# First batch of attention: p turned by plain transposes, reciprocals of the sums multiplied into x by GpSimd

## Chip, cores and metric

One core of one Trainium2 chip. The metric is the device time of one launch in microseconds, as the median over runs. The engines are PE (TensorE, matmuls), DVE (VectorE), ACT (ScalarE), POOL (GpSimd) and SP (SyncE, which issues most of the transfers).

## What is computed

A thresholded attention over 8 batches, 8 heads, 576 rows and a head size of 64, and after it a gated feed-forward block on 4608 rows of 512, with 1536 inner columns. All is float32; the weights arrive as float64 and are taken apart on the chip.

```python
scores = scale * np.matmul(q, k.transpose(0, 1, 3, 2))
thresh = np.max(scores, axis=-1, keepdims=True) - tau
scores = np.where(scores >= thresh, scores, -1000000000.0)
attn = np.exp(scores - np.max(scores, axis=-1, keepdims=True))
attn = attn / (np.sum(attn, axis=-1, keepdims=True) + 1e-09)
x = np.matmul(attn, v)          # then (B,H,S,D) -> (B*S, H*D)
g = x @ w_gate
out = (g * (1.0 / (1.0 + np.exp(-g))) * (x @ w_val)) @ w_out
```

## The kernel before

The kernel has two parts. The first batch is written out by hand, in the order in which the program issues its instructions; the seven others are handed out by a planner (`Plan`), which keeps a modelled time for each engine and places jobs by the durations that stand in their calls. Engines run their own instructions strictly in that order.

The first batch has four pairs of heads and, in each, five tiles of query rows: four of 128 and one of 64. The tiles 0 and 1 ("early", `t < TA`) of all four pairs come first, as their rows of x feed the first unit of the feed-forward block; the tiles 2, 3 and 4 follow, pair by pair. Beside them the weights are brought into float32 piece by piece: ACT splits (L322, L323), POOL clamps (L315), DVE shifts (L342) and joins (L348), POOL adds the lower part (L358). From the second round on, PE fills in gate and value matmuls of the first unit (L580), with the tanh halves copied by ACT (L595, L596), the value product on DVE (L604) and the gate product on POOL (L611).

One tile passes through these steps. PE makes the scores of both heads in the two PSUM tiles `sc` (L462, L468 for the last tile). DVE takes the negated maxima (L479), ACT the exponentials into p (L482) and the threshold (L484), DVE masks p and sums it (L487), adds the sums up and takes the reciprocals `ri` (L489, L490). While the next tile is in its first steps, p is turned: PE writes four blocks of 128 columns for each head to a PSUM bank `tp`, and the 64 columns left over of both heads to a bank `end`; ACT copies them to `pT` and `pT2` (L540, L544, L547). One tile later PE multiplies with v (`attend_tile`, L564, L566) into a bank `xa`, from which ACT copies x to its place (L569), the moving operand of the gate matmuls.

The division by the sums happens in one of two ways. For early tiles the turning is a true matmul against the identity scaled by `ri` (ACT makes it, L503; PE at L533 and L537). For the others p itself is scaled, one head by ACT (L497), the other by POOL (L495), and turned by plain transposes (L531, L539); for the scores of the second head there, the key columns start 64 further on (`turned`), so that the 64 columns left over of both heads lie side by side and one transpose turns both.

The four PSUM banks for `tp`, `end`, `xa`, `pg` and `pv` go round in the order in which they are given back (`bank`, `give_back`). A bank is written again only when its last reader is done; so are the two `sc` tiles, which DVE's mask reads last.

In the planned part two tiles of the first batch are still attended, in its first two groups; the second goes through the planner as a job of ACT.

Of the kernel before, what the change touches and what calls it, by code (L numbers as in the profile page):

```python
# [13 lines left out]
AF = mybir.ActivationFunctionType  # L14
ALU = mybir.AluOpType
# [113 lines left out]
def kernel(  # L129
# [105 lines left out]
    def room(n):  # L235
        nonlocal at
        at += n
        return pall[:, at - n:at]
# [6 lines left out]
    dbufs = deque(room(2 * P).rearrange("p (h q) -> p h q", h=2) for _ in range(2))  # L245
# [199 lines left out]
    heads = [slice(h * D, (h + 1) * D) for h in range(2)]  # L445

    def turned(t):
        return TA <= t < NT

    def statistics(*names):  # L450
        return [stp.tile([P, 2 * MU, 2] if x == "mx" else [P, 2 * MU], F32, name=x) for x in names]
# [1 line left out]
    def scores(seg, t):  # L453
        qT, kT = seg["qT"], seg["kT"]
        q0 = t * P - seg["q0"]
        if t < NT:
            pss = [next_sc() for _ in range(2)]
            for h, hs in enumerate(heads):
                cut_ = D if turned(t) and h == 1 else 0
                for n, lo, to in [(0, 0, D), (0, D, SH), (1, 0, SH)] if cut_ else [(0, 0, SH), (1, 0, SH)]:  # L460
                    at_ = (n * SH + lo - cut_) % S
                    nc.tensor.matmul(pss[h][:, n, lo:to], qT[hs, q0:q0 + P], kT[hs, at_:at_ + to - lo],  # L462
                                     start=True, stop=True)
        else:
            pss = [next_sc()]
            for n, h in ((0, 0), (1, 1), (1, 0), (0, 1)):
                hs = heads[h]
                nc.tensor.matmul(pss[0][hs, n, 0:SH], qT[hs, q0:q0 + D], kT[hs, n * SH:(n + 1) * SH],  # L468
                                 start=True, stop=True)
        nm, th, ri, tot = statistics("nm", "th", "ri", "tot")  # L470
        sm = sums[0]
        sums.rotate(1)
        m = len(pss)
        scs = [ps[:, :, 0:SH] for ps in pss]
        both = pbufs[0].rearrange("p h s -> p (h s)")[:, KM:KM + P]
        ps = [pbufs[0][:, x, :].rearrange("p (n s) -> p n s", n=2) for x in range(m)]
        pbufs.rotate(1)
        for x in range(m):
            nc.vector.tensor_reduce(out=nm[:, x:x + 1], in_=scs[x], axis=AX.XY, op=ALU.max, negate=True)  # L479
        yield  # L480
        for x in range(m):
            nc.scalar.activation(ps[x], scs[x], AF.Exp, bias=nm[:, x:x + 1])  # L482
            if x == 0:
                nc.scalar.activation(th[:, 0:m], nm[:, 0:m], AF.Identity, bias=cut, scale=-1.0)  # L484
        yield
        for x in range(m):
            nc.vector.scalar_tensor_tensor(out=ps[x], in0=scs[x], scalar=th[:, x:x + 1], in1=ps[x],  # L487
                                           op0=ALU.is_ge, op1=ALU.mult, accum_out=sm[:, x, 0:1])
        nc.vector.tensor_reduce(out=tot[:, 0:m], in_=sm[:, 0:m, 0:3:2], axis=AX.X, op=ALU.add)  # L489
        nc.vector.reciprocal(out=ri[:, 0:m], in_=tot[:, 0:m])  # L490
        units = [ident] * m
        if t >= TA:
            for x in range(m):
                if x % 2:
                    nc.gpsimd.tensor_scalar(out=ps[x], in0=ps[x], scalar1=ri[:, x:x + 1], scalar2=None, op0=ALU.mult)  # L495
                else:
                    nc.scalar.activation(ps[x], ps[x], AF.Copy, scale=ri[:, x:x + 1])  # L497
# [16 lines left out]
    def flip_steps():  # L514
        if not unflipped:
            return
        seg, t, both, ps = unflipped.popleft()
# [5 lines left out]
        for h, (p, unit) in enumerate(ps):  # L523
            tp = bank("tp")
            if h == len(ps) - 1:
                end = bank("end")
            for kt in range(KT):
                at_ = kt * P + (D if turned(t) and h == 1 else 0)
                ks, to = slice(at_, at_ + P), slice(kt * P, (kt + 1) * P)
                if unit is ident:  # L530
                    nc.tensor.transpose(tp[:, to], p[:, ks], unit)  # L531
                else:
                    nc.tensor.matmul(tp[:, to], p[:, ks], unit, start=True, stop=True)  # L533
            if t < NT:
                if h == 1 and not turned(t):
                    for hs, (p_, unit_) in zip(heads, ps):
                        nc.tensor.matmul(end[hs, 0:P], p_[:, KM:S], unit_, start=True, stop=True)  # L537
                elif h == 1:
                    nc.tensor.transpose(end[:, 0:P], both, unit)  # L539
                nc.scalar.copy(pT[:, h], tp.rearrange("p (t q) -> p t q", q=P))  # L540
            else:
                for hs in heads:
                    nc.tensor.matmul(end[hs, 0:D], p[hs, KM:S], unit[hs, hs], start=True, stop=True)
# [3 lines left out]
        nc.scalar.copy(pT2, end[:, 0:n])  # L547
        give_back(end)
        unattended.append((seg, t, pT, pT2))

    def attend_tile(copy=lambda xa, fn: (fn(), give_back(xa))):
        if not unattended:
            return
        if not xts:
            for u, lo in enumerate((0, 2 * XW)):
                xts["full", u] = xall[:, lo:lo + XW].rearrange("p (c n) -> p c n", c=NCC)
            xts["last", 0] = xlast
        seg, t, pT, pT2 = unattended.popleft()
        vr, vr2 = seg["v"]
        n = pT2.shape[1]  # L560
        xa = bank("xa")
        for kt in range(KT):
            for h in range(2):
                nc.tensor.matmul(xa[h * D:(h + 1) * D, 0:n], vr[:, h, kt, :], pT[:, h, kt, :],  # L564
                                 start=(kt == 0), stop=False)
        nc.tensor.matmul(xa[:, 0:n], vr2, pT2, start=False, stop=True)  # L566
        u, lo = divmod(t * P, TC)
        to = xts[("last", 0) if t == NT else ("full", u)][:, seg["i"], lo:lo + n]
        copy(xa, lambda: nc.scalar.copy(to, xa[:, 0:n]))  # L569

    ungated = []
    GR = 2
# [1494 lines left out]
    for z, (n, x) in enumerate((n, x) for n in range(len(halved)) for x in range(NU3)):  # L2067
# [112 lines left out]
```

## Time and profile before

| | us |
|---|---|
| median of 3 runs | 1370.39 |
| lowest and highest run | 1369.83, 1373.53 |
| span of the profiled execution | 1368.2 |
| first batch, from the start to its last scores of PE in the planned part | about 133 |
| PE busy in the span | 1348.9 |
| DVE, ACT, POOL busy in the span | 1090.6, 866.7, 714.2 |

The busy time of a group of instructions is the time in which at least one of them runs; what an engine waited for stands behind it in brackets, as "idle before <- releaser". A line such as L495 is the line of the kernel before. A float32 matmul appears as two records, a transpose as one. Matmuls overlap in the array, so the time of one record is longer than the step from one to the next; steps are read from the starts.

### The profile page before, as it was taken

The numbers are of one execution on the slowest core, as the hardware profiler recorded it, in microseconds if no ns is written. First come the engines' busy times: TensorE is split into PE (matmuls) and PEld (weight loads), VectorE is DVE, ScalarE is ACT, GpSimd is POOL, SyncE is SP. The second block draws the span as 40 slices with busy tenths as digits, with TensorE's granted clock in tenths as the row PEclk, the third lists the DMA queues.
The fourth block names the chain that finished last, engine by engine and source line by source line (L and its number), as shares of the span: only waits on it lengthen the run. The fifth ranks groups of instructions, "written<-read, shape, count | busy, mean of one in ns | idle before, by whom it ended". The sixth has DMA issues, their size and how long they took to land.

```text
span 1368.2 us, 39123 instructions
## 1 busy us (share of the span) xinstructions
PE 1348.9 (99%) x15590; PEld 1126.1 (82%) x15590; DVE 1090.6 (80%) x2860; ACT 866.7 (63%) x2218; POOL 714.2 (52%) x664
## 2 busy tenths in 40 slices
PE   9999999999999999999999999999999999999998
PEld 7777887777788788878887788888887788999888
DVE  6788998888877778887878877887888776797786
ACT  6788765767765767677767676677767674330330
POOL 2688698754655669434972487437843592000000
PEclk9999999999999999999999999999999999999999
DMA  8752414466425440654154514543255404423411
GB/s 173 184 204 71 102 37 137 115 184 174 120 52 157 135 105 27 193 153 113 37 171 129 160 25 135 157 142 68 69 161 145 111 27 155 150 78 139 162 54 32
DMA packets 208293, 162.31 MB, mean 119 GB/s; under 512 B 166128, under 2 KB 180464, under 8 KB 202736
## 3 DMA queue, kind: packets, MB, share of 16 engines
q1 hardware_dynamic: 203920, 158.86, 41.2%
q8 instruction: 123, 2.02, 0.6%
q10 hardware_dynamic: 4192, 0.95, 0.3%
q14 instruction: 58, 0.48, 0.1%
HBM read 138.28 MB, written 21.50 MB: 117 GB/s over the span
## 4 chain that ended last, share of the span: by engine, by line
PE 89%; DVE 4%; POOL 2%; DMA 1%; issue 1%; SPq 1%; ACT 1%; ACTq 0%; DVEq 0%; POOLq 0%
PE pb L1021 17%; PE pa L1021 12%; PE px L1510 12%; PE sc L1770 10%; PE pe L1021 9%; PE xa L1904 9%; PE po L1303 5%; PE py L1519 5%; PE pg L1234 1%; PE sc L1188 1%; PE pv L1234 1%; PE pe L1188 1%; PE sc L1021 1%; POOL pall L495 1%; SPq L391 1%
## 5 line engine op out<-in xcount | busy, mean ns | idle before, releaser
L1846 ACT ACTIVATE pall<-sc,nm 128x288 f32<-128x288 f32 x504 | 234.2, 500 | 78.2 <-DVE pall L1848 42.5
L1848 DVE SCALAR_TENSOR_TENSOR pall<-sc,th,pall 128x288 f32<-128x288 f32 x504 | 243.7, 513 | 38.4 <-ACT pall L1846 21.9
L1021 PE MATMUL pb<-xall,big 128*128 128x256 f32 x1104 | 262.0, 380 | 0.0
L1021 PEld LDWEIGHTS pb<-xall,big 128*128 128x128 f32 x1104 | 207.5, 190 | 29.6 <-issue 1.6
L1883 DVE STREAM_TRANSPOSE pall<-pall 128x576 f32<-128x576 f32 x252 | 188.1, 764 | 28.9 <-POOL pall L1878 15.5
L1881 ACT ACTIVATE pall<-pall,ri 128x288 f32<-128x288 f32 x416 | 190.5, 526 | 22.8 <-DVE ri L1869 22.0
L1021 PE MATMUL pa<-xall,big 128*128 128x256 f32 x752 | 178.9, 381 | 0.3 <-ACT sc L1028 0.3
L1021 PEld LDWEIGHTS pa<-xall,big 128*128 128x128 f32 x752 | 140.7, 190 | 20.9 <-issue 2.5
L872 POOL TENSOR_TENSOR hall<-hall,tmp 128x512 f32<-128x512 f32 x80 | 102.5, 1281 | 104.9 <-DVE hall L1080 64.3
L1770 PE MATMUL sc<-kT,qT 64*32 64x288 f32 (+1 forms) x5376 | 145.5, 345 | 0.1
L1805 DVE TENSOR_REDUCE mx<-sc 128x2 f32<-128x576 f32 x168 | 118.4, 746 | 34.0 <-PE sc L1770 33.1
L1878 POOL TENSOR_SCALAR pall<-pall,ri 128x288 f32<-128x288 f32 x88 | 87.9, 1006 | 104.4 <-DVE ri L1869 75.4
L1021 PE MATMUL pe<-xall,big 128*128 128x256 f32 x576 | 138.4, 383 | 0.9 <-ACT pall L1881 0.9
L1770 PEld LDWEIGHTS sc<-kT,qT 64*32 64x32 f32 x5376 | 98.2, 106 | 49.9 <-issue 10.6
L1904 PE MATMUL xa<-pall,vall 64*32 64x288 f32 x4032 | 129.6, 404 | 3.0 <-PE px L1510 2.7
L1021 PEld LDWEIGHTS pe<-xall,big 128*128 128x128 f32 x576 | 107.6, 190 | 19.7 <-issue 4.3
L1904 PEld LDWEIGHTS xa<-pall,vall 64*32 64x32 f32 x4032 | 83.3, 107 | 42.0 <-issue 5.0
L872 POOL TENSOR_TENSOR tmp<-tmp 128x512 f32<-128x512 f32 x36 | 45.8, 1273 | 84.9 <-ACT tmp L1102 84.9
L1863 ACT COPY sums<-sums 32x6 f32<-32x6 f32 x336 | 66.6, 198 | 28.0 <-DVE pall L1848 23.9
L1079 ACT ACTIVATE vall<-tmp 128x512 f32<-128x512 f32 x96 | 60.0, 628 | 34.0 <-DVE tmp L1092 27.2
L1519 PE MATMUL py<-wo,hall 128*128 128x256 f32 x336 | 74.8, 379 | 0.0
L872 POOL TENSOR_TENSOR hall<-hall 128x384 f32<-128x384 f32 (+2 forms) x67 | 67.4, 1018 | 8.9 <-PE px L1510 8.2
(272 smaller groups left out, 2509.2 us busy)
## 6 DMA issues: line engine op xcount, KB each, us to landing
big<-sums_hbm SPq DMA_DIRECT2D x42, 1024.0 KB, 5.2
big<-sums_hbm SPq DMA_DIRECT2D x48, 768.0 KB, 4.6
vall<-in_v_dram SPq DMA_DIRECT2D x112, 144.0 KB, 3.1
out_dram<-big SPq DMA_DIRECT2D x32, 256.0 KB, 3.1
qT<-in_q_dram SPq DMA_DIRECT2D x112, 72.0 KB, 4.7
kT<-in_k_dram SPq DMA_DIRECT2D x112, 72.0 KB, 3.0
wo<-in_moe_w_gate_dram SPq DMA_DIRECT2D x16, 384.0 KB, 3.8
wo<-in_moe_w_val_dram SPq DMA_DIRECT2D x16, 384.0 KB, 4.7
```

Source lines behind the costliest of these rows:

```text
L872: return lambda: nc.gpsimd.tensor_tensor(out=out, in0=a, in1=b, op=op)
L1021: nc.tensor.matmul(ps[:, i], w[:, k_, i * P:(i + 1) * P], x[:, k_, :], start=first and i == k_ == 0, stop=True, skip_group_check=True)
L1510: nc.tensor.matmul(ps, a[:, f, :], ws[n][:, f, :], start=bank_ not in begun, stop=True, skip_group_check=True)
L1519: nc.tensor.matmul(ps(), a[:, f, i * P:(i + 1) * P], operands[o][:, f, :], start=first and f == 0, stop=True, skip_group_check=True)
L1770: nc.tensor.matmul(to[g * G:(g + 1) * G], qT[hs, col:col + G], kT[hs, c * SH + lo:c * SH + hi], start=True, stop=True)
L1805: rs.append(job("DVE", 0.72 if w > 1 else 0.42, lambda h=h: nc.vector.tensor_reduce(out=mx[:, n0 + h:n1 + h + 1:max(2, n1 - n0), 0], in_=s ...
L1846: ej = job("ACT", 0.44, lambda x=x, n=n: nc.scalar.activation(ps[x], scs[x], AF.Exp, bias=nm[:, n:n + 1]), ej, rank=top, on=on[x])
L1848: masks[x] = job("DVE", 0.48, lambda x=x, n=n: nc.vector.scalar_tensor_tensor(out=ps[x], in0=scs[x], scalar=th[:, n:n + 1], in1=ps[x], op0 ...
L1878: scaled.append(job("POOL", 1.02, lambda x=x, n=n: nc.gpsimd.tensor_scalar(out=x, in0=x, scalar1=ri[:, n:n + 1], scalar2=None, op0=ALU.mul ...
L1881: scaled.append(job("ACT", 0.46, lambda x=x, n=n: nc.scalar.activation(x, x, AF.Copy, scale=ri[:, n:n + 1]), rj, rank=rank))
L1883: seg["turned"].append(job("DVE", 0.72, lambda both=both: nc.vector.transpose(out=both, in_=both), *scaled, rank=rank))
L1904: nc.tensor.matmul(holds[a].ap()[x * G:(x + 1) * G, 0:SH].rearrange("d (i q) -> d i q", q=G), vr[rs, h, j, ds], p[rs, h, :, j, :], start=( ...
```

## The change

p is no longer scaled. All tiles of the first batch are turned by plain transposes, and the scores of early tiles, too, have the shifted key columns of the second head. The scaled identities and both scalings of p are gone. In place of them `attend_tile` writes a second half to the bank `xa`: for each head a matmul whose stationary operand is `ri` of that head, repeated in 64 columns, and whose moving operand is the identity. That gives the reciprocals of the tile's rows, along the columns, in every row of the head. ACT copies both halves to SBUF (one of two buffers, in the room of the scaled identities), and POOL multiplies them into x. The planner's duration for the ACT job of the last tile goes from 0.27 to 0.39.

```diff
     def turned(t):
-        return TA <= t < NT
+        return t < NT
...
         nc.vector.reciprocal(out=ri[:, 0:m], in_=tot[:, 0:m])
-        units = [ident] * m
-        if t >= TA:
-            for x in range(m):
-                if x % 2:
-                    nc.gpsimd.tensor_scalar(out=ps[x], in0=ps[x], scalar1=ri[:, x:x + 1], scalar2=None, op0=ALU.mult)
-                else:
-                    nc.scalar.activation(ps[x], ps[x], AF.Copy, scale=ri[:, x:x + 1])
+        unflipped.append((seg, t, both, [p.rearrange("p n s -> p (n s)") for p in ps], ri[:, 0:m]))
         yield
-        if t < TA:
-            units = [dbufs[0][:, x, :] for x in range(m)]
-            dbufs.rotate(1)
-            for x in range(m):
-                nc.scalar.activation(units[x], ident, AF.Copy, scale=ri[:, x:x + 1])
-        unflipped.append((seg, t, both, [(p.rearrange("p n s -> p (n s)"), unit) for p, unit in zip(ps, units)]))
         yield
...
             for kt in range(KT):
-                at_ = kt * P + (D if turned(t) and h == 1 else 0)
-                ks, to = slice(at_, at_ + P), slice(kt * P, (kt + 1) * P)
-                if unit is ident:
-                    nc.tensor.transpose(tp[:, to], p[:, ks], unit)
-                else:
-                    nc.tensor.matmul(tp[:, to], p[:, ks], unit, start=True, stop=True)
+                at_ = kt * P + (D if t < NT and h == 1 else 0)
+                nc.tensor.transpose(tp[:, kt * P:(kt + 1) * P], p[:, at_:at_ + P], ident)
             if t < NT:
-                if h == 1 and not turned(t):
-                    for hs, (p_, unit_) in zip(heads, ps):
-                        nc.tensor.matmul(end[hs, 0:P], p_[:, KM:S], unit_, start=True, stop=True)
-                elif h == 1:
-                    nc.tensor.transpose(end[:, 0:P], both, unit)
+                if h == 1:
+                    nc.tensor.transpose(end[:, 0:P], both, ident)
...
         xa = bank("xa")
+        for h, hs in enumerate(heads):
+            one, of = (ri[:, h:h + 1], ident) if t < NT else (ri[:, 0:1], ident[:, hs])
+            nc.tensor.matmul(xa[hs, n:2 * n], one.broadcast_to((P, D)), of, start=True, stop=True)
...
-        copy(xa, lambda: nc.scalar.copy(to, xa[:, 0:n]))
+        both = rbufs[0][:, 0:2 * n]
+        rbufs.rotate(1)
+
+        def weigh():
+            nc.scalar.copy(both, xa[:, 0:2 * n])
+            nc.gpsimd.tensor_tensor(out=to, in0=both[:, 0:n], in1=both[:, n:2 * n], op=ALU.mult)
+
+        copy(xa, weigh)
...
-            j = job("ACT", 0.27, box[1], m, rank=0)
+            j = job("ACT", 0.39, box[1], m, rank=0)
```

In the changed kernel the transposes stand at L517 and L520, the new matmuls at L545, the attend matmuls at L548 and L550, the copy at L557 and the product at L558.

More of the change, by code (lines that the diff above doesn't have):

```diff
@@ L244 @@
     make_identity(nc, ident)
-    dbufs = deque(room(2 * P).rearrange("p (h q) -> p h q", h=2) for _ in range(2))
+    rbufs = deque(room(2 * P) for _ in range(2))
     ones = room(TC)
@@ L516, in flip_steps @@
             return
-        seg, t, both, ps = unflipped.popleft()
+        seg, t, both, ps, ri = unflipped.popleft()
         n = P if t < NT else D
@@ L522, in flip_steps @@
         end = None
-        for h, (p, unit) in enumerate(ps):
+        for h, p in enumerate(ps):
             tp = bank("tp")
@@ L542, in flip_steps @@
                 for hs in heads:
-                    nc.tensor.matmul(end[hs, 0:D], p[hs, KM:S], unit[hs, hs], start=True, stop=True)
+                    nc.tensor.matmul(end[hs, 0:D], p[:, KM:S], ident[:, hs], start=True, stop=True)
                 nc.scalar.copy(pT, tp.rearrange("p (t h q) -> p h t q", h=2, q=D))
@@ L548, in flip_steps @@
         give_back(end)
-        unattended.append((seg, t, pT, pT2))
+        unattended.append((seg, t, pT, pT2, ri))
     def attend_tile(copy=lambda xa, fn: (fn(), give_back(xa))):
@@ L557, in attend_tile @@
             xts["last", 0] = xlast
-        seg, t, pT, pT2 = unattended.popleft()
+        seg, t, pT, pT2, ri = unattended.popleft()
         vr, vr2 = seg["v"]
```

## The prediction

> **What bounds the kernel now.** I read the page first: the span, then the chain of work that ended last by engine. Then I cut the span into stages by their windows, and read the first 138 us engine by engine in the timeline.
>
> ```profile
> span 1368.2 us, 39123 instructions
> ...
> PE 89%; DVE 4%; POOL 2%; DMA 1%; issue 1%; SPq 1%; ACT 1%; ACTq 0%; DVEq 0%; POOLq 0%
> ```
>
> ```profile
> 36.00:39.30 3.30, 1.10 (x11) 0.74 (x9) 3.30 (x5) 2.62 (x7) 2.41 (x3) 1.00 0.86 271
> 39.30:46.10 6.80, 6.63 (x32) 5.25 (x33) 5.87 (x17) 4.33 (x10) 4.98 (x4) 0.50 0.91 239
> ...
> 80.80:100.40 19.60, 18.55 (x141) 14.26 (x141) 16.23 (x31) 17.18 (x32) 16.71 (x12) 1.00 0.77 268
> ...
> 175.00:300.00 125.00, 124.90 (x1674) 99.53 (x1658) 109.02 (x319) 83.54 (x231) 95.66 (x91) 1.00 0.43 121
> ```
>
> A window row gives its length, the busy time of PE, weight loads, DVE, ACT, POOL, then PE's clock. From 175 us PE is never idle, so it carries the rest of the span as one rigid block: whatever the first batch wins or loses before about 138 us arrives at the end unchanged. The planned part keeps its order on every engine; only the first batch is edited. There no engine is full: between 80.8 and 100.4 us PE is busy 18.55, ACT 17.18, POOL 16.71 and DVE 16.23 of 19.60 us. That is a loop of waits, to be priced wait by wait.
>
> Before 39.5 us the loads set the pace:
>
> ```profile
> 32.00 2.45 DMA vall<-in_v_dram
> ...
> 39.47 3.02 PE L462 MATMUL sc<-pall,qT 64*128 64x288 f32 x8 [2.37 <-DVE pall L487]
> ```
>
> The chain comes out of a DMA at 34.45; DVE then turns that head's keys and queries, in order ahead of the maxima, and PE sits idle 2.37 us for the mask. PE work saved before this point widens that hole and buys nothing.
>
> **The change part by part.** Gone are eight GpSimd and twelve ScalarE scalings of p (L495, L497) and sixteen scaled identities (L503). Added are, in each of twenty tiles, two matmuls ri x identity, a copy of xa twice as wide, and a GpSimd product.
>
> ```profile
> L495 POOL TENSOR_SCALAR pall<-pall,ri x8: 1867/1874/2022, 59.2 to 127.9; 128x576 f32<-128x576 f32 x8
> ...
> L497 ACT ACTIVATE pall<-pall,ri x12: 760/784/924, 62.1 to 134.2; 128x576 f32<-128x576 f32 x12
> ...
> L569 ACT COPY xall<-xa 128x128 f32<-128x128 f32 x16 | 4.7, 293 | 3.6 <-PE xa L566 3.6
> ...
> L1915 ACT COPY xall<-xa 128x256 f32<-128x256 f32 x56 | 20.7, 381 | 17.3 <-PE xa L1904 17.2
> ...
> L358 POOL TENSOR_TENSOR big<-big x10: 1806/1818/2461, 35.3 to 106.6; 128x768 uint32<-128x768 uint32 x10
> ...
> L872 POOL TENSOR_TENSOR xall<-xall 128x256 f32<-128x256 f32 x52 | 36.8, 728 | 2.8 <-ACT xall L1915 1.3 <-ACT xlast L1916 0.4
> ```
>
> The wider copy costs 0.381 - 0.293 = 0.09 us more. No row shows a GpSimd product of 128x128: half of 728 ns, 0.36, bounds it below and 0.73 above; I take 0.45, near the lower end, since half the elements and one start remain. POOL loses 8 x 1.87 = 15.0 us and gains at most 20 x 0.45 = 9.0; ACT loses 12 x 0.78 = 9.4 and more. Both end lighter.
> PE's prices:
>
> ```profile
> 47.76 1.25 PE L462 MATMUL sc<-pall,qT 64*128 64x288 f32 x8
> 49.03 1.42 DVE L479 TENSOR_REDUCE nm<-sc 128x1 f32<-128x576 f32 x2 [2.13 <-PE sc L462]
> 50.41 2.05 PE L533 MATMUL tp<-pall 128*128 128x128 f32 x16
> 51.49 0.82 DVE L487 SCALAR_TENSOR_TENSOR pall<-sc,th,pall 128x576 f32<-128x576 f32 x1 [0.17 <-ACT th L484]
> 52.39 0.44 PE L537 MATMUL end<-pall 128*64 128x128 f32 x4
> 52.76 1.70 PE L462 MATMUL sc<-pall 64*128 64x288 f32 x10
> ```
>
> ```profile
> 82.83 0.69 PE L564 MATMUL xa<-big,vall 128*64 128x64 f32 x16
> ...
> 88.08 1.09 PE L564 MATMUL xa<-big,vall 128*64 128x128 f32 x16
> ...
> 103.29 1.04 PE L531 MATMUL tp<-pall 128*128 128x128 f32 x8
> ...
> 104.28 1.03 PE L580 MATMUL pg<-xall,big 128*128 128x256 f32 x4
> ```
>
> An early flip against a scaled identity takes 52.76 - 50.41 = 2.35 us (16 + 4 records); a flip by plain transposes 104.28 - 103.29 = 0.99. So each early tile saves 1.36. The two new matmuls are four records into alternating column halves, like L564: 4 x 1.09/16 = 0.27, in the last tile 4 x 0.69/16 = 0.17; L537, of the same shape, bounds it above by 0.44 and it cannot be below 0.
>
> The product also stands between x and the first gate matmuls. There the last tile's x is needed by the fourth of four matmuls, six records of 1.03/4 after the first: 1.5 us, which cover a copy of 0.38 and a product of 0.45. If POOL is held then by a weight sum (L358), up to 1.8 us come on top, once; I take nothing.
>
> Now the sum, from scores to scores (sc), each by the engine that ends last:
>
> 39.47 to 47.76: PE is the bound (DVE then idles 2.13). The clock is at half for most of it, so the matmuls cost about 0.54; the flip comes last, and I price it at full clock: -1.36 + 0.54 = **-0.8**.
>
> 47.76 to 52.76: PE would need 5.00 - 1.36 + 0.27 = 3.91, but DVE takes over: its mask starts 3.73 after the scores, lasts 0.82, and only then may the next scores write. 5.00 becomes 4.55: **-0.45**. Most of the 1.36 is lost here.
>
> 52.76 to 62.71: here ACT sets the pace.
>
> ```profile
> 55.94 0.27 ACT L569 COPY xall<-xa 128x128 f32<-128x128 f32 x1 [0.26 <-PE xa L566]
> ...
> 62.71 1.36 PE L462 MATMUL sc<-pall 64*128 64x288 f32 x10
> ```
>
> The copy of xa stands ahead of the exponentials in ACT's queue and waits for PE; behind it wait the exponentials, the copies of the turned p, and PE's second attend. The new matmuls and the wider copy both delay it: 0.27 + 0.09 = **+0.36**.
>
> 62.71 to 73.80: one wait for L495 against one pair of matmuls, 0. Then:
>
> ```profile
> 73.80 1.36 PE L462 MATMUL sc<-pall 64*128 64x288 f32 x10
> ...
> 75.85 0.56 DVE L342 TENSOR_SCALAR big<-big 128x768 uint32<-128x768 uint32 x1 [0.72 <-POOL big L315]
> ...
> 80.81 2.09 PE L462 MATMUL sc<-pall 64*128 64x288 f32 x10 [0.72 <-DVE pall L487]
> ```
>
> POOL's clamp is late because L495 stood ahead of it; without it POOL is 1.87 - 0.45 = 1.4 earlier and DVE's wait goes: **-0.72**.
>
> 80.81 to 132.9, three segments alike:
>
> ```profile
> 86.96 1.19 PE L468 MATMUL sc<-pall 64*64 64x288 f32 x8
> ...
> 90.87 0.66 PE L531 MATMUL tp<-pall 128*128 128x128 f32 x4 [0.68 <-POOL pall L495]
> ...
> 93.73 1.36 PE L462 MATMUL sc<-pall 64*128 64x288 f32 x10
> ...
> 100.38 2.09 PE L462 MATMUL sc<-pall 64*128 64x288 f32 x10 [0.36 <-DVE pall L487]
> ```
>
> ```profile
> PEld tp L531 <- POOL pall L495: 2.5, 3, 0.9
> ```
>
> PE's three waits for the scaled p, 2.5 us as the weight loads see them, vanish, against 3 x 0.27: **-1.7**. The iteration after it (93.73 to 100.38) gains nothing more: DVE goes from the gate product through its queue to the mask, however early PE is (its rows stand with the first rival). The one before it is PE's and pays 3 x 0.17: **+0.5**.
>
> 132.9 to 147: the matmuls delay transposes whose copies free a PSUM bank, 0.27, and the last tile 0.17: **+0.44**.
>
> ```profile
> 137.31 3.72 PE L1234 MATMUL pg<-xall,big 128*128 128x256 f32 x16 [0.58 <-ACT big L547]
> ```
>
> No DMA moves. SP's store of the last rows waits for POOL in place of ACT, with nothing pressing behind it. The extra split of the early scores costs 0.05 at most.
>
> Sum: -0.8 - 0.45 + 0.36 - 0.72 - 1.7 + 0.5 + 0.44 = -2.4. The profiled span, 1368.2, becomes 1365.8. The median of the runs, 1370.39, lies 2.2 above the span; I carry that over: **1368.0**.
>
> **The rivals.**
>
> Everything runs up to PE (more gain). In the segment above PE idles where the sum gives it nothing: 100.38 waits for the mask, and its 2.09 us for ten records against 1.36 at 93.73 are another wait. DVE is slow there for one reason:
>
> ```profile
> 78.06 1.96 DVE L348 SCALAR_TENSOR_TENSOR big<-wo,big 128x768 uint32<-128x768 uint32 x2
> ...
> 93.83 0.69 DVE L604 SCALAR_TENSOR_TENSOR hall<-tmp,pv 128x512 f32<-128x512 f32 x1 [1.16 <-PE pv L580]
> ...
> 96.71 2.88 DVE L348 SCALAR_TENSOR_TENSOR big<-wo,big 128x768 uint32<-128x768 uint32 x2
> ...
> 96.64 1.27 POOL L611 TENSOR_TENSOR hall<-hall,tmp 128x512 f32<-128x512 f32 x1
> ```
>
> At 96.71 two joins take 2.88 beside a POOL product, at 78.06 they took 1.96. If a lighter POOL runs that product before them, DVE wins about 1 us in each of three segments: 1365.0. Against it: POOL's product waits for a ScalarE split that moves little.
>
> POOL's new products hold DVE (slower). That row shows a price: a two-input GpSimd instruction cost a DVE join about 1 us. The change swaps one-input scalings for twenty two-input products. If each of the sixteen after 39.5 us holds DVE its 0.45 on the path, that is 7.2 against a gain of 2.4: 1375.2; from the sixth on the kernel is slower. Against it: DVE's waits (1.16, 2.13 above) are slack, and the products come while DVE mostly reads PSUM. The Trainium skill, page "SBUF — State Buffer", section "SBUF: two separate sides", states it as an exclusive lock of a port pair between GpSimd and a DVE instruction with two SBUF inputs; the 2.88 agrees.
>
> A second stretch at half clock. PE's hole at 36 to 39.3 us (1.10 busy of 3.30) is followed by 6.8 us at a clock of 0.50, in which an iteration took 8.29 in place of 5.00. Shorter flips make PE's holes wider; one more such stretch costs 3.3: 1371.3. Against it: the other waits of PE quoted here are under 1 us each. The Trainium skill, page "TensorE: Matmul & The Clock Gate", section "Part 1: The HAM clock gate", gives the rule: free-running windows of about 3.4 us, an idle one halves the clock. Its phase differs from run to run, so by it the cost can also move the other way.
>
> The change frees what nobody needed. POOL's and ACT's time is given back where DVE already decides, the L495 waits return as waits on the copies: 1370.4.
>
> **How the numbers follow.** The forecast 0.42, with its own range 1366 to 1370; all up to PE 0.23; products hold DVE 0.10; second half-clock stretch 0.12; nothing 0.13. About 0.3% (4.1 us) is what a measurement of this kernel tells from no change. Faster by that means below 1366.3: most of the first rival and a little of the forecast, 0.29. Slower means above 1374.5: most of the POOL rival, 0.08. The rest 0.63. The new matmuls enter the sum with 0.54 + 0.27 + 0.81 + 0.51 + 0.44 = 2.6: at nothing the forecast is 1365.4, at L537's price (0.44/0.27 as much) 1369.6. The range 1363.5 to 1372.5 takes in both, the first rival and part of it with cheap matmuls, and a good half of the POOL rival.
>
> **What would show it.** Right: no wait of a transpose on POOL; flips of 0.99 throughout; scores 47.76 to 52.76 at about 4.55; 80.81 to 100.38 shortened from 19.57 by about 0.4; the first planned gate matmuls near 135; the same rows after it. Wrong: DVE joins or shifts of 1.5 us and more beside L558's products (the new GpSimd line), a second window at 0.50, a gate matmul waiting for POOL, or transposes that wait for ScalarE.

## The result, and the profile after

The changed kernel takes 1368.32 us (median of 20 runs, 1365.27 to 1371.09), the kernel before 1372.02 (20 runs, 1368.09 to 1375.92). The ratio is 0.9976, 95% interval 0.9967 to 0.9985: 3.3 us faster, below the 0.3% that the prediction called its limit. Run again on another occasion, it took 1366.96 beside 1369.28, 0.9982 (0.9968 to 0.9996).

The page of the changed kernel, its span and its chain:

```profile
span 1366.5 us, 39110 instructions
...
PE 91%; DVE 4%; DMA 2%; SPq 1%; ACT 1%; issue 1%; ACTq 0%; DVEq 0%
```

POOL has gone from the chain, PE has 91% in place of 89%. The matmuls of the first batch, from the timeline of PE (start, length, records, and in brackets the idle time before and its releaser):

```profile
39.76 3.24 PE L462 MATMUL sc<-pall,qT 64*128 64x288 f32 x10 [3.74 <-DVE pall L487]
...
46.90 1.36 PE L462 MATMUL sc<-pall,qT 64*128 64x288 f32 x10
...
51.25 2.09 PE L462 MATMUL sc<-pall 64*128 64x288 f32 x10 [0.34 <-DVE pall L487]
53.27 0.44 PE L545 MATMUL xa<-pall,ri 128*64 128x128 f32 x4
...
57.45 1.58 PE L548 MATMUL xa<-big,vall 128*64 128x128 f32 x16 [1.10 <-ACT big L521]
...
61.99 1.36 PE L462 MATMUL sc<-pall 64*128 64x288 f32 x10
...
72.50 1.36 PE L462 MATMUL sc<-pall 64*128 64x288 f32 x10
...
79.01 2.09 PE L462 MATMUL sc<-pall 64*128 64x288 f32 x10
...
128.93 1.72 PE L1761 MATMUL sc<-kT,qT 64*32 64x288 f32 x64
133.59 3.72 PE L1225 MATMUL pg<-xall,big 128*128 128x256 f32 x16 [0.58 <-ACT big L528]
...
143.34 0.87 PE L1225 MATMUL pg<-xall,big 128*128 128x256 f32 x3
```

The same matmuls stood at 39.47, 47.76, 52.76, 62.71, 73.80, 80.81, 132.87, 137.31 and 146.94 before. So the first batch is 3.6 us ahead at 146.94 (in the second profile 4.0), where 2.4 were predicted. No transpose waits for POOL any more. The windows of both kernels from the second scores of the late tiles on, before and then after, each 84 to 85 us long:

```profile
62.70:147.00 84.30, 79.69 (x700) 61.48 (x700) 69.57 (x142) 71.24 (x139) 68.50 (x45) 1.00 0.46 141
```

```profile
62.00:147.00 85.00, 84.05 (x764) 66.87 (x764) 73.67 (x149) 68.60 (x134) 61.59 (x51) 1.00 0.51 152
```

PE idled 4.6 us there before and idles 0.95 now: the loop of waits has become a stage that PE fills.

Not all of the 3.6 us arrives. The spans differ by only 1.7. The planned part in the timelines of PE, before and then after:

```profile
341.18 1.70 PE L1770 MATMUL sc<-kT,qT 64*32 64x288 f32 x64
343.81 1.99 PE L1021 MATMUL pe<-xall,big 128*128 128x256 f32 x8 [0.93 <-ACT pall L1881]
...
784.01 1.70 PE L1770 MATMUL sc<-kT,qT 64*32 64x288 f32 x64
...
1126.73 1.72 PE L1770 MATMUL sc<-kT,qT 64*32 64x288 f32 x64
```

```profile
780.74 1.41 PE L1761 MATMUL sc<-kT,qT 64*32 64x288 f32 x40
783.33 0.69 PE L1761 MATMUL sc<-kT,qT 64*32 64x144 f32 x24 [1.18 <-issue]
...
1125.07 1.72 PE L1761 MATMUL sc<-kT,qT 64*32 64x288 f32 x64
```

At 780.74 the lead is still 3.27. Then PE stops in the middle of one block of 64 score records, for 1.18 us with no releaser in the profile, and the block takes 1.58 us longer than before; at 1125.07 the lead is 1.66. The prediction called the planned part "one rigid block". Such a stop is called a stand below; it is measured as the time by which a block of scores and what follows it takes longer than the same block in most of the other profiles.

### The profile page after: what moved, and what is told of

The parts are those of the page before. It is cut to its first block, busy times and chain, and to the rows that moved or that the text cites. A ratio compares the mean times of both kernels' runs of the same rounds, so it can differ in the third digit from the quotient of the medians.

```text
span 1366.5 us, 39110 instructions
## 1 busy us (share of the span) xinstructions
PE 1346.2 (99%) x15598; PEld 1124.6 (82%) x15598; DVE 1094.1 (80%) x2860; ACT 857.4 (63%) x2190; POOL 710.8 (52%) x676
## 4 chain that ended last, share of the span: by engine, by line
PE 91%; DVE 4%; DMA 2%; SPq 1%; ACT 1%; issue 1%; ACTq 0%; DVEq 0%
PE pb L1012 17%; PE pa L1012 12%; PE px L1501 12%; PE sc L1761 10%; PE pe L1012 9%; PE xa L1895 9%; PE po L1294 5%; PE py L1510 5%; PE sc L1179 1%; PE sc L462 1%; PE pe L1179 1%; PE pg L1225 1%; PE pv L571 1%; PE sc L1012 1%; PE pg L571 1%
```

## The experiments

Twelve experiments in three groups of four rows, each of twelve runs (no product: six). Each group has its own runs of the kernel before, 29, 35 and 35 of them: 1370.82, 1369.28 and 1369.01 us. A lead is how much earlier than before the same matmul of PE starts in the two profiles. A profile shows one execution: for no product, early tiles again and exponentials first it is the run with the longest time, for early tiles only the one with the shortest. So leads and medians can't be set against each other row by row.

| | median us | ratio to before, 95% interval | lead at 146.94 | lead at 1126.73 |
|---|---|---|---|---|
| early tiles only | 1372.54 | 1.0019, 1.0008 to 1.0030 | 2.8 | 0.6 |
| late tiles only | 1366.19 | 0.9970, 0.9958 to 0.9981 | 3.5 | 3.2 |
| no product | 1364.94 | 0.9959, 0.9945 to 0.9972 | 2.8 | 2.4 |
| new matmuls twice | 1369.28 | 0.9995, 0.9984 to 1.0007 | 1.8 | 0.0 |
| the change again | 1366.96 | 0.9982, 0.9968 to 0.9996 | 4.0 | 2.9 |
| the change, hole filled | 1369.41 | 1.0000, 0.9986 to 1.0014 | 1.3 | -1.8 |
| before, hole filled | 1369.62 | 1.0002, 0.9989 to 1.0016 | 3.5 | 0.9 |
| late tiles only, hole filled | 1365.75 | 0.9975, 0.9961 to 0.9989 | 5.9 | 5.3 |
| the change, 18 idle products more | 1367.80 | 0.9990, 0.9978 to 1.0002 | 5.7 | 4.4 |
| the change, 42 idle products more | 1370.18 | 1.0009, 0.9997 to 1.0021 | 2.1 | -0.4 |
| early tiles only, again | 1371.99 | 1.0024, 1.0012 to 1.0036 | -0.3 | -4.4 |
| exponentials first | 1367.41 | 0.9984, 0.9972 to 0.9997 | 0.9 | 0.2 |

The lead before 147 us swings by up to 3 us between two profiles of one kernel, and 0.3 to 4.1 us of it are lost between the two columns (the two versions with late tiles only lose 1.1 and 1.2 more soon after the second). Both had to be explained before the totals could be read.

### Which tiles gain

Early tiles only: the late ones keep both scalings of p and have neither the new matmuls nor the product.

```diff
+        if t >= TA:
+            for x in range(m):
+                if x % 2:
+                    nc.gpsimd.tensor_scalar(out=ps[x], in0=ps[x], scalar1=ri[:, x:x + 1], scalar2=None, op0=ALU.mult)
+                else:
+                    nc.scalar.activation(ps[x], ps[x], AF.Copy, scale=ri[:, x:x + 1])
...
-        copy(xa, weigh)
+        copy(xa, weigh if t < TA else lambda: nc.scalar.copy(to, xa[:, 0:n]))
```

> Only the early tiles (0 and 1) go the new way; the tiles 2, 3 and 4 have p scaled by ScalarE and GpSimd and no reciprocal matmuls, as before. Theory (waits on the path, priced one by one): the early steps of the changed kernel sum to +0.29 - 1.15 - 0.65 + 0.79 = -0.7 us against the kernel before, so a ratio of about 0.9995; scores 39.5 to 52.8 shorter by 1.8, 52.8 to 62.7 longer by 0.8, and the three waits of the transposes for the scaled p are back with 2.5 us in all. Rival (the gain is TensorE work saved by plain transposes, 8 tiles x 1.36 us): most of the 3.3 us stays, ratio below 0.998.

Late tiles only: the early ones keep the scaled identities.

```diff
     def turned(t):
-        return t < NT
+        return TA <= t < NT
...
+        if t < TA:
+            units = [dbufs[0][:, x, :] for x in range(m)]
+            dbufs.rotate(1)
+            for x in range(m):
+                nc.scalar.activation(units[x], ident, AF.Copy, scale=ri[:, x:x + 1])
...
-        copy(xa, weigh)
+        copy(xa, weigh if t >= TA else lambda: nc.scalar.copy(to, xa[:, 0:n]))
```

> Only the tiles 2, 3 and 4 go the new way; the early tiles are turned against scaled identities as before. Theory (waits on the path): the late steps of the changed kernel sum to -0.59 - 0.50 - 2.14 + 0.34 = -2.9 us, ratio about 0.998, with no wait of a transpose on GpSimd. Rival (plain transposes of early tiles carry the gain): under -1 us, ratio above 0.999.

The late tiles alone took 0.9970, the early ones alone 1.0019: the late part carries the gain, the theory of the second run holds; for the first neither the theory nor the rival fits. It was run again to see where it loses.

> The early tiles in the new form and the late ones scaled as before, once more: its time was 1372.5 beside 1370.8, while its one profile stood 2.8 us ahead of the kernel before at 147 us and 0.6 ahead at the end, and took 1369.7, the least of its twelve. Theory: the lead at 147 us comes and goes with the stretch at half clock (in that profile from 7.9 to 11.2 and from 35.6 to 38.7, in the load-bound part, none after 39), and a typical execution has it after 39 us: lead at 147 us near -0.5, as the two terms of the early tiles make it, and 1.5 to 2 us lost at TensorE's stands in the planned part; ratio 1.001 to 1.003. Rival: the early part by itself is slower: scores at 39.5 us late by 1 us or more, or steps between 39 and 63 longer than before's 23.2 us.

It took 1.0024. The profile at the ends of its parts, from the timeline of PE:

```profile
39.78 3.07 PE L462 MATMUL sc<-pall,qT 64*128 64x288 f32 x10 [1.55 <-DVE pall L487]
...
494.64 0.71 PE L1768 MATMUL sc<-kT,qT 64*32 64x144 f32 x28 [1.13 <-issue]
...
1131.17 1.72 PE L1768 MATMUL sc<-kT,qT 64*32 64x288 f32 x64
```

The stretch that lasts from 62.71 to 146.94 before, 84.23 us, takes 84.27 here, and the scores at 39.78 are 0.3 late: the first batch is as fast as before, so the rival falls. In this execution, the longest of the twelve, the loss comes after 147 us, 4.1 us of lead, most of it at four stands (0.6, 1.55, 0.6 and 0.95 us at 307, 491, 931 and 1002 us of the kernel before, against its own one of 1.0). The theory is right about the place and too small about the size. Part of the two medians is the half clock, treated below: the mean granted clock of the runs is 0.9959 and 0.9967, and 0.9984 and 0.9989 in the kernel before beside them.

### Where PE stands in the planned part

In the second profile of the change the stand at 783 us came back, smaller:

> The changed kernel as it is, so that the next three and the earlier four have one with which they share a chip. Before the change 1370.8 in the earlier comparison, the changed kernel 1368.3: 0.9976 is expected, 0.9967 to 0.9985. What the profile is for: in the changed kernel's profile TensorE ran at half clock from 18.5 to 21.9 us and from 39.0 to 45.8, before only from 39.3 to 46.2; in the one with the early tiles alone from 7.9 to 11.2 and from 35.6 to 38.7. Theory: the lighter early tiles leave TensorE more idle, so the clock halves once more before 39 us, at another place in each execution, and part of the gain is lost there: another stretch at half clock before 39 us, at an other place. Rival: the stretch at 18.5 was an accident of one execution: none before 39 us.

```profile
780.45 1.41 PE L1761 MATMUL sc<-kT,qT 64*32 64x288 f32 x40
782.21 0.69 PE L1761 MATMUL sc<-kT,qT 64*32 64x144 f32 x24 [0.35 <-issue]
...
1123.87 1.72 PE L1761 MATMUL sc<-kT,qT 64*32 64x288 f32 x64
```

It stops after the same 40 records. Without the product, and with the exponentials first, PE has the same instructions as in the change, and both stand at this place too (0.76 and 0.72 us longer than before). The two versions with the new form in late tiles only stand at 1077 instead, and again behind the block at 1127, at 1148 us of the kernel before (one also at 637, the other at 890), and the new matmuls twice at 307, 491, 890 and 931. To tell the program from the work, the six idle products at the very start of the change, done at 5.9 us, were cut into more and smaller ones:

```diff
-    run_idle(6)
+    ps = bank("idle")
+    for _ in range(24):
+        nc.tensor.matmul(ps[0:32, 0:64], ones[:, 0:32], ones[:, 0:64], start=True, stop=True)
+    give_back(ps)
```

> The changed kernel with the six idle products at its very start (done at 5.9 us, before the first scores at 7.4) cut into 24 of a quarter of the columns: 18 products more, about as much TensorE time, nothing else moved. In two profiles of the changed kernel TensorE stood at the same one place of the planned part, the scores at 784 us, 1.58 and 0.75 us longer than in kernels with another number of instructions, once with nothing in the profile that released it; the versions with scaled identities stood at 1077 and 1127 us instead. Theory: where TensorE's instructions fall in the program sets where it stands, so with 18 more the place at 784 goes or another comes, with 0.5 to 1.6 us each, while the steps up to 147 us stay within 0.3; the time differs from the changed kernel's (1368.3 and 1367.0) by anything within 2 us. Rival: the place belongs to the work (its loads, its operands): the stand at 784 us stays.

The second has 48 products of 32 columns:

> The same with the six idle products cut into 48 of an eighth of the columns: 42 products more. Theory: the stands at other places again than with none and with 18 more, the sum of them anywhere from 0 to 3 us, and the time by as much apart. Rival: a stand at 784 us, the time within 0.7 us of that with 18 more.

Timeline of PE with 18 more, then with 42 more:

```profile
337.21 0.72 PE L1764 MATMUL sc<-kT,qT 64*32 64x144 f32 x31 [0.97 <-issue]
...
778.77 1.70 PE L1764 MATMUL sc<-kT,qT 64*32 64x288 f32 x64
```

```profile
490.84 0.71 PE L1764 MATMUL sc<-kT,qT 64*32 64x144 f32 x27 [0.21 <-issue]
```

On the stands the theory holds: with 18 more the block at 778.77 runs through in 1.70 us, and PE stands at 337, 633 and 1074; with 42 more at 307, 491, 931 and 1002, the very places of the early tiles alone. One part of it misses: the steps up to 147 us should have stayed within 0.3, but with 18 more the lead there is 5.7, mostly as the half clock after 39 us lasts 3.4 us in place of 6.8.

Neither the loads nor the data of these blocks differ. What moves the places is the number of instructions that PE has had. Counted from the start, PE stops near 784 us after 9460 of its records in both profiles of the change, and after 9460 or 9459 with the hole filled, the exponentials first and no product. The filled one has 14 records more in front, and stops 14 records earlier in its block. With the new matmuls twice and with 42 more, two different programs, it stops after 5665 and after 11485 records in both; with the early tiles alone after 5532 and 11352, 133 fewer each time, which with a weight load for every record is 266 instructions.

The sum of the stands is 1.6 and 0.75 us in the two profiles of the change, 2.6 with 18 more, 2.3 to 3.7 us in the four profiles with the places of the early tiles alone, and 1.0 in the kernel before (behind the block at 341.18; there the profile names ACT, yet with 18 more PE stops inside the same block with no releaser). That puts 1 to 2 us between programs that do the same work. The medians with 18 and with 42 more lie 2.4 us apart, but not by their stands, 2.6 and 2.3: the granted clock of their runs is 0.9970 and 0.9958 in the mean, by estimate up to 0.0012 x 1368 = 1.6 us, and in its profile only the second has a half clock before 39 us.

What does PE wait for? The page of the change has this row among its DMA queues:

```profile
q8 instruction: 123, 2.02, 0.6%
```

These are 123 packets of 16 KB that bring instructions, for 15598 matmul records of PE and as many weight loads, 254 for each packet. In the trace one of them starts at 780.92 and lands 0.88 us later; PE goes on at 783.33, 1.53 us after that. Behind 147 us the fourteen profiles have 25 waits of PE of 0.2 us or more without a releaser, and every one of them ends 1.24 to 1.61 us after such a packet has landed. So does the one behind 341.18 in the kernel before (1.50). For waits with a releaser that all versions have, such as 0.53 us at 520 us, that time is anything from 0.6 to 15 us. So the stands go with the fetch of instructions. That PE waits for the packet, and not for something else that comes with it, isn't shown. The Trainium skill, page "Runtime: NRT & Kernel Launch", section "Instruction fetch mechanics", has instructions streamed in blocks of 256, with the cost at a block's end mostly hidden. The 254 for each packet agree with blocks, and one to five stands, of 0.2 to 1.6 us, among 123 packets agree with mostly hidden.

Open is a further 0.8 to 1.1 us that some profiles (both of the change) lose between 200 and 300 us without a stand.

### The half clock

The prediction named a hole of PE and the half clock behind it. A few idle products were put into it, seven in the change, four in the kernel before and in the late tiles only.

```diff
+            if n == NP - 1 and x == 0:
+                run_idle(7)
             go = scores(seg, t)
```

> The changed kernel with seven idle products of TensorE (operands on chip, result unused) ahead of the scores at 39.8 us, in the hole from 36 to 39.8. Theory: the stretch at half clock from 39.0 to 45.8 is ordered by that hole and costs about half of itself, 3.3 us, since TensorE is busy throughout it: no half clock after 39 us, scores 39.76 to 46.90 in about 4.4 instead of 7.1, and 2.5 us off the changed kernel's time, ratio to before about 0.9958. Rival: the loads or VectorE hold 39 to 47 anyway (its scores wait for VectorE's pall): the clock stays full and the scores still come near 46.5, ratio 0.9972 to 0.998.

> The kernel before with four idle products of TensorE at the same place (its hole is shorter, 37.1 to 39.5). Theory of the clock: 39.47 to 47.76 becomes about 5.5 instead of 8.3, ratio 0.998 (2.5 us faster). Rival: VectorE and the loads hold it: under 1 us, ratio over 0.9993.

> Late tiles in the new form, early tiles by scaled identities as before, and four idle products in the hole ahead of the scores at 39 us. Without the idle products this took 1366.2 beside 1370.8 (0.9970). Theory: the gains add, 4.1 + 2.5 us, ratio about 0.995. Rival: the stretch at half clock costs nothing that the loads wouldn't: 0.997.

Timeline of PE in the kernel before with four, then in the change with seven:

```profile
37.59 1.99 PE L265 MATMUL idle<-pall 128*128 128x256 f32 x8 [0.53 <-ACT xall L569]
39.51 1.25 PE L462 MATMUL sc<-pall,qT 64*128 64x288 f32 x8
...
49.36 1.65 PE L462 MATMUL sc<-pall 64*128 64x288 f32 x10
```

```profile
39.50 4.97 PE L265 MATMUL idle<-pall 128*128 128x256 f32 x14 [1.89 <-ACT pall L557]
44.41 1.36 PE L462 MATMUL sc<-pall,qT 64*128 64x288 f32 x10
```

In the kernel before it does what the theory of the clock says, and more: no half clock until the launch ends, and 39.47 to 52.76, 13.29 us, becomes 9.85. In the change the idle products wait for a PSUM bank, start only at 39.50 and hold the scores up until 44.41: a miss of the experiment. Still the totals don't follow. The filled kernel before is 3.5 us ahead at 146.94 and 0.9 at 1126.73, and its median is 1.0002; the filled late tiles come to 0.9975, not to the 0.995 of the theory.

The mean granted clock of every run says more than the one profile. Of the 35 runs of the kernel before in this group, 14 ran at 1.000 and took 1367.8 us in the mean; the 12 at 0.997 or 0.998 took 1371.2. So the half clock goes with some 3.4 us of the total, about what the theory gave the stretch, but many executions don't have it. Filled, 10 of 12 ran at 1.000, yet they took 1369.9, 2 us more than the unfilled kernel at the same clock. In its one profile the stands, at 341 and 784 us, are 1.33 and 1.32, against 1.0 in the kernel before: the eight records of the idle products move the stands too. For the total the rival's number is right, and its reason is not.

The half clock also comes earlier. In seven of the ten profiles with light early tiles (the new form there) a stretch lies before 36 us, in none of the four with scaled identities. The change again is one of the three without, as its rival said. The runs agree: of 122 with light early tiles none ran at a mean clock of 1.000, of the twelve with late tiles only five did. The change has 0.9962 and 0.9967 in the mean, and the kernel before beside the second 0.9988. Windows of the early tiles alone (second run), then of its PE timeline, then of PE in the kernel before:

```profile
12.70:16.10 3.40, 1.87 (x13) 1.25 (x12) 3.04 (x7) 1.97 (x5) 0.00 (x0) 1.00 1.16 223
16.10:23.70 7.60, 7.60 (x40) 6.32 (x41) 5.71 (x15) 4.91 (x10) 2.18 (x3) 0.55 0.90 237
```

```profile
14.21 0.27 PE L526 MATMUL end<-pall 128*128 128x128 f32 x1
16.01 2.22 PE L462 MATMUL sc<-pall,qT 64*128 64x288 f32 x8 [1.53 <-DVE pall L487]
```

```profile
15.24 0.44 PE L537 MATMUL end<-pall 128*64 128x128 f32 x4
16.10 1.98 PE L462 MATMUL sc<-pall,qT 64*128 64x288 f32 x8 [0.42 <-DVE pall L487]
```

The shorter flip ends a microsecond sooner, the scores come no sooner, so the hole is 1.53 in place of 0.42 us; a window of 3.4 us with 1.87 busy is followed by 7 us at half clock. The second profile of the change has the same hole, 1.52, and no half clock. It goes with where the hole falls. Take the twelve profiles that have a half clock in the first 60 us, and cut that time into windows of 3.41 us, the length of the shortest stretch, counted from the start of a half clock. All 13 windows in which PE is busy for 1.86 us or less are followed at once by half clock; of the eight with 1.87 to 2.01 us five are, and above 2.05 us one is (2.4, in the first profile of the change). In five profiles the 1.5 us hole lies inside one window, in which PE is then busy for 1.86 to 1.89 us. In the second profile of the change two windows share it (2.80 and 2.51).

The price: without such a stretch the scores of the fourth pair come at 38.51, 38.63 and 38.91 (18 more, matmuls twice, the change again), after one at 17 to 24 us at 39.76, 39.78, 40.17, 40.28 and 41.02 (the change, early tiles again, exponentials first, 42 more, no product). With scaled identities they come at 38.88 to 39.94 (four profiles). So the light early tiles come some 0.7 us sooner when the clock holds, and up to 1.6 later than in the kernel before when it doesn't.

### The single costs

No product: the copy is narrow again, POOL multiplies nothing, x is not divided.

```diff
-            nc.scalar.copy(both, xa[:, 0:2 * n])
-            nc.gpsimd.tensor_tensor(out=to, in0=both[:, 0:n], in1=both[:, n:2 * n], op=ALU.mult)
+            nc.scalar.copy(to, xa[:, 0:n])
```

> The changed kernel without the GpSimd product and with the narrow copy of xa: x of the first batch is not divided by its sums; the reciprocal matmuls stay. Theory (products are hidden, GpSimd and VectorE have slack): within 1 us of the changed kernel, that is 2.5 to 4.5 us faster than before; VectorE's busy time falls by up to 3.5 us without moving the scores. Rival (the products hold VectorE on the path): 3 us or more faster than the changed kernel, 6 us or more faster than before.

From scores 61.99 to the gate matmuls at 143.34 it takes 80.93 us, the change 81.35: product and wide copy cost 0.42 us over twelve tiles. In the first batch the theory holds. The total is 5.9 us below the kernel before by the medians, outside the theory's 2.5 to 4.5 and just short of the rival's 6. With stands of 0.76 in the one and 0.75 to 1.58 in the other the rest isn't settled.

New matmuls twice:

```diff
-        for h, hs in enumerate(heads):
+        for h, hs in [*enumerate(heads)] * 2:
```

> The changed kernel with each reciprocal matmul issued twice: 0.27 us more of TensorE in every tile, 0.17 in the last of a pair, 5.0 in all. Theory: about half of it lies on the path (iterations that TensorE sets, 0.27 each), so 2 to 3 us slower than the changed kernel and within 1.5 us of the kernel before. Rival (TensorE idles enough in the first batch to hide it): under 1 us slower than the changed kernel.

From 51.25 to 143.34 it takes 93.81 us in place of 92.09: 1.72 for fourteen tiles, 0.12 each. The total fits the theory, 0.9995 beside the 0.9976 of the change; but its stands, at the places of the early tiles alone, are larger than the change's, so the total doesn't measure the matmuls.

Exponentials first, in late segments too:

```diff
-            if n < NP:
-                attend_tile(lambda *y: box.extend(y))
-            else:
-                attend_tile()
+            attend_tile(lambda *y: box.extend(y))
```

> The changed kernel with the exponentials of the next tile ahead of the copy of xa on ScalarE in late segments too (in the changed kernel the copy goes first there). The prediction put that order at +0.36 between 52.76 and 62.71, and before to after that stretch grew by 0.79. Theory: the wait of the gate and of the scores' masks goes, 51.25 to 61.99 becomes shorter by 0.3 to 0.5; the copy that follows is later by 1.4 us, but what reads it (the gate at 60) is not; ratio within 0.0004 of the changed kernel's. Rival: the product on GpSimd then comes later and the flips or joins behind it wait: some later step between 62 and 147 grows by 0.5 us or more.

```profile
52.67 2.09 PE L462 MATMUL sc<-pall 64*128 64x288 f32 x10 [0.58 <-DVE pall L487]
...
62.12 1.24 PE L462 MATMUL sc<-pall 64*128 64x288 f32 x9
...
104.75 1.56 PE L571 MATMUL pv<-xall,big 128*128 128x256 f32 x6 [0.42 <-ACT pall L557]
106.24 0.94 PE L468 MATMUL sc<-pall 64*64 64x288 f32 x6
```

This is PE's timeline. The stretch becomes 9.45 us in place of 10.74, so the theory is right that the order costs there. But later value matmuls wait for the copy, 99.09 to 106.24 grows from 6.27 to 7.15, and to 143.34 it loses 2.6 us again. The rival is right that a later step grows by more than 0.5; what waits, by the row at 104.75, is a matmul for the copy, not for the product. Used for the one stretch alone it might win 1 us; that wasn't run.

No version beats the change by more than the intervals.

## Why the prediction was right or wrong

1368.0 was predicted and 1368.3 measured, with the direction and the size class right. Behind it errors cancel, and the hit is in part luck: the first batch gains more than the sum said, and the planned part gives back what the sum took as safe. The start of the sum moved as well: 1370.39 was the median of three runs, and beside the change the kernel before took 1372.02. The gain was 3.3 us there, and 2.3 by the medians the second time, where 2.4 were said. Step by step, from scores to scores, in the two profiles of the change:

| | predicted | first | second |
|---|---|---|---|
| to 39.47 | 0 | +0.29 | -0.56 |
| 39.47 to 47.76 | -0.8 | -1.15 | -0.71 |
| 47.76 to 52.76 | -0.45 | -0.65 | -0.65 |
| 52.76 to 62.71 | +0.36 | +0.79 | +0.79 |
| 62.71 to 73.80 | 0 | -0.58 | -0.58 |
| 73.80 to 80.81 | -0.72 | -0.50 | -0.50 |
| 80.81 to 132.87 | -1.7 + 0.5 | -2.14 | -2.15 |
| 132.87 to 146.94 | +0.44 | +0.34 | +0.34 |
| sum | -2.4 | -3.6 | -4.0 |

"PE work saved here buys nothing": wrong both ways. It buys up to 1 us when the clock holds and costs up to 1.6 where the wider holes halve it. The rival of a second stretch at half clock thus did come true, in most of the profiles, but at a place where the prediction had not looked: it weighed the holes after 39 us, and the shortened flips before that had widened one.

39.47 to 52.76: right. DVE took over, as the new wait of 0.34 for the mask shows, and 4.35 us came where 4.55 was said.

52.76 to 62.71, PE's timeline of before:

```profile
54.39 1.09 PE L564 MATMUL xa<-big,vall 128*64 128x128 f32 x16
```

The mechanism, the copy ahead of the exponentials, is right, and its size too: from the new matmuls at 53.27 to the scores at 61.99 the change takes 8.72 us where the kernel before took 8.32 (54.39 to 62.71), +0.40. Missed is that the wait for the mask, which the step before gained from, is paid inside the next scores: their ten records take 2.09 us in place of 1.70. Counted together, the two steps give +0.14 against a predicted -0.09.

62.71 to 73.80, "one wait for L495 against one pair of matmuls, 0": wrong. The timeline of PE before, then after:

```profile
69.44 0.49 PE L566 MATMUL xa<-big,vends 128*128 128x128 f32 x2
69.95 0.66 PE L531 MATMUL tp<-pall 128*128 128x128 f32 x4
70.97 0.63 PE L531 MATMUL tp<-pall 128*128 128x128 f32 x4 [0.36 <-issue]
...
71.54 2.32 PE L580 MATMUL pv<-xall,big 128*128 128x256 f32 x10
```

```profile
68.94 0.49 PE L550 MATMUL xa<-big,vends 128*128 128x128 f32 x2
69.27 1.04 PE L517 MATMUL tp<-pall 128*128 128x128 f32 x8
...
70.25 2.32 PE L571 MATMUL pv<-xall,big 128*128 128x256 f32 x10
```

From the end of the attend to the value matmuls it was 2.10 us, and is 1.31. The wait for the scaled p cost 0.8, split in two parts, of which the larger carries the label "issue". (The prediction's 2.6 for all new matmuls also leaves out the pair in this stretch.) A list of waits by releaser shows only a part of such a wait; the step between two starts shows all of it.

73.80 to 80.81: right in kind; 0.50 of 0.72, since the pair of new matmuls in it was left out.

80.81 to 132.87: mis-sized by 0.9. By iteration, in the first profile: the three with the wait for the scaled p gain 2.13 where 1.7 was said, the three ahead of them pay 0.36 where 0.5 was said, and the two that were to gain nothing gain 0.18 and 0.19. The new matmuls were priced too high, 1.3 us in the two terms: doubled, they cost 0.80 in the whole stretch (50.72 us against 49.92). The waits were longer than the 2.5 us of their row: from the end of the attend to the value matmuls it was 2.37, 2.39 and 1.94 us, and is 1.31, 1.30 and 1.31. And the first rival's mechanism is there too, in part. The timelines of POOL and of DVE after:

```profile
93.93 1.27 POOL L602 TENSOR_TENSOR hall<-hall,tmp 128x512 f32<-128x512 f32 x1
```

```profile
94.35 2.53 DVE L348 SCALAR_TENSOR_TENSOR big<-wo,big 128x768 uint32<-128x768 uint32 x2
```

The gate product starts ahead of the two joins, no longer with them, and they take 2.53 us in place of 2.88: 0.35 of the 1 us that the rival hoped for in each segment.

132.87 to 146.94: right, with the same wait of 0.58.

POOL's product, estimated at 0.45:

```profile
L558 POOL TENSOR_TENSOR xall<-pall 128x128 f32<-128x128 f32 x16 | 9.3, 583 | 2.3 <-ACT pall L557 2.3
```

This row is a group of the changed kernel; the mean is 583 ns. It does hold DVE back now and then (the join at 81.99 takes 2.04 us, the same one 1.24 without the product), but all of it, with the wide copy, costs 0.42 us in the late tiles, where the rival charged 0.45 for each of sixteen. That rival falls.

"From 175 us on PE is never idle, so it carries the rest of the span as one rigid block": this is the step that failed. The block is rigid in its order, not in its time. Of 3.6 and 4.0 us of lead 1.7 and 2.9 were left at 1126.73. Some 1.3 and 1.4 us go before 300 us, without a stand, and their cause stays open. After that the places of the stands count, which go with the number of PE's instructions, and the change has eight matmul records more: the stand of the kernel before at 341 us gives 1.0 back, and the change's own at 784 us takes 1.6 and 0.75.

## What to carry to other kernels

Price a removed wait by the step between the starts around it, not by the row of its releaser, and follow a saving into the next step, which may hand part of it back. Before making a load-bound stage lighter on PE, look at what the wider holes do to its clock. When two versions of a long program differ by a few tenths of a per cent, shift the program by a few harmless instructions first: if the time moves as much, the comparison isn't about the edit. Look at the granted clock of every run too, and not only of the one with a profile.

## What the runs showed of the hardware

PE stood for 0.2 to 1.6 us in the middle of dense blocks of score records, at places that moved when 18 or 42 idle products were added 300 us and more ahead; the change with 42 more stood at the same four places as the early tiles alone, another program. In all profiles together, the 25 waits of PE of 0.2 us or more without a releaser, behind 147 us, ended 1.24 to 1.61 us after a 16 KB packet of the instruction queue had landed.

Runs of the kernel before at a mean granted clock of 1.000 took 1367.8 us (14 runs), those at 0.997 or 0.998 took 1371.2 (12 runs).

A window of 3.4 us in which PE was busy for 1.87 was followed by 7 us at half clock in one profile, and the same hole by none in another; the Trainium skill, page "TensorE: Matmul & The Clock Gate", section "Part 1: The HAM clock gate", speaks of free-running windows, with which that agrees, and of an idle window, where here one busy for 55% was enough. All 13 windows with PE busy for 1.86 us or less, counted as above, were followed by half clock. Eight records of idle products (1.99 us) in a hole of 2.4 us kept the clock at 1.00.
